# A fused attention and two-expert kernel: the written order of all its steps made anew

## The chip, the cores and the metric

The kernel runs on one core of a Trainium2 chip. The metric is the device time of one execution in microseconds (us); below are the median and the ends of three executions. A core has five engines that run side by side, each in the order of its own program: TensorE (PE, matrix products; PEld is its weight loads), VectorE (DVE), ScalarE (ACT), GpSimd (POOL) and SyncE (SP), which here issues all DMA transfers. They wait for one another by semaphores, so that an instruction that waits holds up everything behind it on its engine.

## What is computed

Causal attention with a bias from running sums of `s`, over 4 batches of 8 heads, 576 rows and 64 columns, and then two feed-forward blocks over all 2304 rows of 512 columns. The reference, cut:

```
scores = np.matmul(q, k.transpose(0, 1, 3, 2)) / sqrt(64)
cum = np.cumsum(np.maximum(s, 0.0), axis=-1)
bias = -(cum[:, :, :, None] - cum[:, :, None, :])
scores = np.where(causal, -1e9, scores + np.minimum(bias, 0.0))
attn = softmax(scores);  x = attn @ v              # heads side by side: 2304 x 512
h = x @ w_in;  x2 = (h - tanh(h)) @ w_out          # expert 1, d_ff 2048
h = x2 @ w2_in;  solu = h * softmax(h)             # expert 2, d_ff 1024
out = (layernorm(solu) * g_ln) @ w2_out
```

The weights come as float64 and are turned into float32 on the chip.

## The kernel before

**Arithmetic.** A float32 factor is split into a high and a low part (`xh`, `xl` in the buffer `xb`; `wih` and `wil`; `woh` and `wol`), and a product is three matmuls: high by high, low by high, high by low. The low part is a difference (`lo`, L831 for the attention's output, `diff`, L313, for the weights). A weight tile comes in as float64 (`cd`, L390) and is turned into float32 by four integer steps on DVE (L399, L402, L405, L410) and one on ACT (L417); then ACT writes the high part (L294) and DVE the low part (L313).

**Attention.** It goes by jobs. A job is a head pair p with some of its nine units; a unit is 64 query rows of both heads. J0 to J3 are pairs 0 to 3 with units 1 to 4 (the first 256 rows), J4 to J7 are pairs 0 to 3 with units 5 to 9, and J8 to J19 are pairs 4 to 15 whole. For each unit PE makes the scores against the keys up to the diagonal (L715; a half of the array for each head) and adds the mask (L723); DVE adds the bias and finds the row's extreme (L732, in buffer `U`); ACT takes the exponential and its sum (L743); DVE guards and inverts the sum (L656, L659); POOL scales the row (L747); PE turns it by transposes against an identity (L781, `idn` or `idx`); ACT copies the turned block to `pt` (L294). When the units of a half are turned, PE weighs the values (L821), ACT and DVE write the result's high and low parts (L294, L831), and SP stores them to DRAM (L834). The bias of J0 to J3 is cumulated in place; that of all others is a table `cum_d` in DRAM, from which SP loads `bc` (L602). Keys come by L580, queries by L584, values by L588 and L590.

**Experts.** Expert 1 goes by nine blocks of 256 rows. Its width of 2048 is 16 slices f of 128; the first eight slices go over all blocks in two visits of four, with the partial sum kept in DRAM, and the last eight after that. For a slice, `h_part` (L868) is 12 matmuls, ACT takes the tanh (L873), DVE the difference, the high and low parts are written to `gh`, and `x2_part` (L891) is 12 matmuls into the bank `acc`. Block 0 takes its `xb` straight from J0 to J3. Expert 2 follows for each block (L1016, L1120, L1134), and the output goes out in L1169.

**What sets the order.** Every piece of work is a step with the engine (or the choice of engines) that may do it, its dependences and the buffers that it takes and frees; there are 3302. `Plan.order` goes through the table `ORDER`: a word in base 36 is three times the step's number plus the choice of engine, and `+n` is n filler matmuls on PE (`warm`, L558, on a tile of zeros `junk`) that yield nothing. The steps go to the engines in the table's order, so the table alone sets what stands ahead of what on each of them. A step's cost, as in `t_score` and `t_turn`, is not looked at on this way. There are 9 buffers `U`, 6 PSUM banks, 4 `bc`, 5 tiles each of keys and queries.

Of the kernel before, what the change touches and what calls it, by code (L numbers as in the profile page):

```python
# [43 lines left out]
TB = 256  # L44
# [5 lines left out]
0 f 3 u i l x 49 4i 7x p r +20 13 10 1u 2i 16 86 1a 1c 1x 39 bu 2l 4d 6 2p 1f 20 3c 4l 2r 23 1i 4f 1l 89 3f 2u 26 2x  # L50
29 bx 3i 81 +7 1o 3l 83 30 1r ff +1 2c 9 3o 2f +1 33 bl 36 +1 3r 3u +1 4r 31x 5i jc 4u 8f 3x 4y 50 5l 32l 8i 8m 5o 53
c 56 96 5r 8o 59 5u 66 8r 40 99 5x 9u 4o 43 9c al 8u 69 46 8x bp 6x 9x 6f a1 br c3 8c a3 5c 70 90 cu 5f a6 c6 c0 73 ca
di 6d a9 6i cx 60 ac 320 6l fc 76 ao e9 d0 6o 79 dl 63 7c af d3 cc 9f d6 9i 6r cf ar ec d9 7f ci f9 6u au 9l ax ef 323
+2 9o cl ei 7i el 93 b0 +2 7l 9r fi 32o 326 eo ai b3 7o 329 j9 co b6 er n9 7r dc cr b9 eu 32c r6 df dr 7u 32r fl bc du
32u 32f bf gc 32x hi 32i dx 330 bi e0 gf 333 fo 339 gi fs 336 jf fu hr fx j6 +7 ji +1 k9 hl g0 ho gl g3 v3 hu gr 11o
gp dp +4 g6 n6 gu hx e3 gx h0 i0 e6 i3 g9 +4 ex h9 if r3 33c h3 hc i6 h6 +1 ii 33f hf v0 33i i9 f0 35x il f3 33l +1 io
ic 3cl ir 33o 33r f6 ki iu 3co km 33u ko n3 jl 3cr jr 33x kc lf 3cu ju jp jx kf 3cx 50l k0 nf kr ix ku lo l6 k3 j0 189
# [1260 lines left out]
```

## Time and profile before

| | us |
|---|---|
| median of three runs | 781.94 |
| lowest, highest | 779.62, 782.77 |
| the profiled execution | 778.94 |
| its span in the trace | 777.2 |
| PE busy | 764.8 (98% of the span) |
| DVE, ACT, POOL busy | 565.0, 409.8, 119.5 |

An engine is busy while it works on an instruction; PE's fillers count as busy too. In a row of the trace the first two numbers are the start and the length, then come the engine, the line, the operation, what it writes and reads, and its shape; a bracket at the end gives the idle time just before and what ended it. The granted clock of PE is 1.00 of full speed in every window. Outside its span the profiled execution has 1.74 us.

### The profile page before, as it was taken

Reading aid. Unit: us, or ns where it says so; the run is one execution under the profiler, and the core shown is the slowest. Engines: PE = TensorE matmul, PEld = TensorE weight load, DVE = VectorE, ACT = ScalarE, POOL = GpSimd, SP = SyncE. Lnnn points to the kernel's source line nnn. Section 1 sums busy time; section 2 is a strip of 40 time slices with the busy share of each in tenths; the row PEclk is TensorE's granted clock in tenths of the full one; section 3 lists DMA queues with packets and bytes.
Section 4 is the critical chain, followed back from the end, with each engine's and each line's share of the span. In section 5 each row is a group of like instructions: output and inputs, shape, how many; then the busy total and the mean of one; then the engine's idle time right before and its main releaser. Section 6 shows DMA issues by size and latency. Waiting matters only on the chain.

```text
span 777.2 us, 16641 instructions
## 1 busy us (share of the span) xinstructions
PE 764.8 (98%) x6239; PEld 676.8 (87%) x6239; DVE 565.0 (73%) x1647; ACT 409.8 (53%) x1030; POOL 119.5 (15%) x193
## 2 busy tenths in 40 slices
PE   8899999999999999999999999999999999999997
PEld 5566788879889899999999898898888899989986
DVE  6888989654564458786699998869496755586783
ACT  6789989775665545454465663423243332343431
POOL 3235354431230200000000000001020001010000
PEclk9999999999999999999999999999999999999999
DMA  7999979874444278876535522112000310110001
GB/s 202 293 302 257 316 235 314 258 209 158 154 140 155 85 252 266 262 261 215 180 123 181 167 83 55 35 48 82 28 28 28 96 55 14 42 55 28 20 36 41
DMA packets 90033, 111.90 MB, mean 144 GB/s; under 512 B 11792, under 2 KB 74256, under 8 KB 89952
## 3 DMA queue, kind: packets, MB, share of 16 engines
q1 hardware_dynamic: 89952, 110.83, 46.2%
q8 instruction: 49, 0.80, 0.4%
q14 instruction: 32, 0.26, 0.1%
HBM read 87.11 MB, written 23.70 MB: 143 GB/s over the span
## 4 chain that ended last, share of the span: by engine, by line
PE 88%; DVE 5%; ACT 2%; DMA 2%; issue 1%; SPq 1%; POOL 0%; DVEq 0%; ACTq 0%; POOLq 0%
PE t L868 23%; PE big L891 13%; PE t L1134 12%; PE acc L891 11%; PE t L821 6%; PE big L1016 6%; PE t L781 5%; PE t L715 5%; PE b L1016 4%; PE t L1120 2%; ACT U L743 1%; DMA bc<-cum_d 1%; DMA cum_d<-pt 1%; ACT pt L294 1%; DVE U L732 1%
## 5 line engine op out<-in xcount | busy, mean ns | idle before, releaser
L868 PE MATMUL t<-xb,wih 128*128 128x256 f32 x1152 | 202.5, 279 | 0.0
L868 PEld LDWEIGHTS t<-xb,wih 128*128 128x128 f32 x1152 | 175.0, 188 | 1.7 <-DVE r L656 0.2
L868 PE MATMUL t<-xb,wil 128*128 128x256 f32 x576 | 159.5, 277 | 0.0
L868 PEld LDWEIGHTS t<-xb,wil 128*128 128x128 f32 x576 | 108.3, 188 | 0.0
L747 POOL TENSOR_SCALAR U<-U,r 128x64 f32<-128x64 f32 (+8 forms) x144 | 82.8, 589 | 163.5 <-DVE r L659 50.2
L891 PE MATMUL acc<-gh,woh 128*128 128x256 f32 x576 | 102.6, 280 | 0.8 <-DVE xp L953 0.7
L891 PE MATMUL big<-gh,woh 128*128 128x256 f32 x576 | 101.0, 278 | 0.0
L873 ACT ACTIVATE th<-t 128x256 f32<-128x256 f32 x144 | 54.7, 381 | 77.1 <-PE t L868 69.7
L877 DVE TENSOR_TENSOR g<-t,th 128x256 f32<-128x256 f32 x144 | 59.5, 417 | 46.6 <-ACT th L873 45.3
L294 ACT CAST gh<-g 128x256 fp32r<-128x256 f32 x144 | 58.1, 406 | 65.1 <-DVE g L877 32.4
L743 ACT ACTIVATE U<-U,m 128x64 f32<-128x64 f32 (+8 forms) x144 | 80.1, 558 | 21.2 <-DVE m L732 20.7
L891 PEld LDWEIGHTS big<-gh,woh 128*128 128x128 f32 x576 | 87.8, 188 | 1.0
L891 PEld LDWEIGHTS acc<-gh,woh 128*128 128x128 f32 x576 | 87.0, 188 | 1.7 <-ACT th L873 0.8
L891 PE MATMUL acc<-gh,wol 128*128 128x256 f32 x288 | 79.8, 277 | 0.4 <-DVE wol L313 0.4
L891 PE MATMUL big<-gh,wol 128*128 128x256 f32 x288 | 79.9, 277 | 0.0
L313 DVE TENSOR_TENSOR gh<-g,gh 128x256 fp32r<-128x256 f32 x124 | 54.0, 439 | 28.2 <-ACT gh L294 27.1
L732 DVE CUSTOM_DVE_ANT_0 U<-bc,t 128x64 f32<-128x64 f32 (+8 forms) x144 | 60.2, 441 | 8.3 <-PE t L723 6.6
L314 POOL TENSOR_TENSOR gh<-g,gh 128x256 fp32r<-128x256 f32 x20 | 16.5, 827 | 316.9 <-ACT gh L294 249.6
L294 ACT COPY pt<-t 128x512 f32<-128x512 f32 (+4 forms) x160 | 60.0, 428 | 7.2 <-PE t L781 6.4
L715 PE MATMUL t<-kn,q 64*64 64x288 f32 (+8 forms) x640 | 58.9, 422 | 2.3 <-DVE wol L313 1.3
L891 PEld LDWEIGHTS acc<-gh,wol 128*128 128x128 f32 x288 | 54.1, 188 | 0.6 <-DVE wol L313 0.6
L891 PEld LDWEIGHTS big<-gh,wol 128*128 128x128 f32 x288 | 54.2, 188 | 0.0
(114 smaller groups left out, 1433.8 us busy)
## 6 DMA issues: line engine op xcount, KB each, us to landing
xb<-xd SPq DMA_DIRECT2D x17, 1024.0 KB, 6.1
cd<-in_moe_w_in_dram SPq DMA_DIRECT2D x24, 512.0 KB, 4.8
cd<-in_moe_w_out_dram SPq DMA_DIRECT2D x24, 512.0 KB, 5.0
bc<-cum_d SPq DMA_DIRECT2D x32, 288.0 KB, 6.4
pd<-xp SPq DMA_DIRECT2D x18, 512.0 KB, 3.8
xp<-pd SPq DMA_DIRECT2D x18, 512.0 KB, 3.6
xd<-xs SPq DMA_DIRECT2D x16, 320.0 KB, 4.5
kn<-in_k_dram SPq DMA_DIRECT2D x16, 288.0 KB, 6.6
```

Source lines behind the costliest of these rows:

```text
L294: then(nc.scalar.copy(o, i) if scale == 1.0 else nc.scalar.activation(out=o, in_=i, func=AF.Copy, scale=scale))
L313: return self.any([("dve", t_dve(n, pair=True), lambda: nc.vector.tensor_tensor(*views(), op), "diff-dve"), ("pool", t_pool(n) + split, la ...
L715: nc.tensor.matmul(X[a][c, :z - a], lhsT=V["q"][r, o:o + 64], rhs=V["k"][r, a:z], start=True, stop=True, skip_group_check=True)
L732: nc.vector.tensor_tensor_reduce(out=X["u"][:, a:z], in0=V["bc"][:, n, a:z], in1=X[b][:, a - b:z - b], scale=-0.125, scalar=X["m"] if "m" ...
L743: nc.scalar.activation(out=X["u"][:, :nk], in_=X["u"][:, :nk], func=AF.Exp, scale=-1.0, bias=X["m"], accum_out=Y["s"][:, n:n + 1])
L747: eng.tensor_scalar(X["u"][:, :nk], X["u"][:, :nk], Y["r"][:, n:n + 1], 1.0, ALU.mult, ALU.mult)
L868: nc.tensor.matmul(ps, lhsT=w[l][:, k, f * 128:f * 128 + 128], rhs=xb[:, r, k, :], start=k == 0 and x == 0, stop=k == 3 and x == 2)
L873: nc.scalar.activation(out=X["th", f], in_=X["h", f], func=AF.Tanh)
L877: nc.vector.tensor_tensor(X["g", f], X["h", f], X["th", f], ALU.subtract)
L891: nc.tensor.matmul(X["acc"][:, m, :], lhsT=w[l][:, f, m * 128:m * 128 + 128], rhs=X["gh", f][:, r, :], start=f == c0 and m % 2 == 0 and x ...
L1016: i = nc.tensor.matmul(o, lhsT=self.x2[j][:, l, x, k], rhs=r[:, b, k, :], start=start and k == 0 and n == 0, stop=k == 1 and n == 2, skip_ ...
L1134: nc.tensor.matmul(X["po"], lhsT=X["lt", k // 4][:, l, k % 4, :], rhs=r[:, k, :], start=k == 0 and a == 0, stop=k == 7 and a == 2)
```

## The change

The table is replaced by another one with the same 3302 steps, and the cost figures in the steps' descriptions are replaced too: those of a score of one part or two, of a turn of one to four blocks, of the weighing (2353 and 801 become 2165 and 685 ns), of an expert-1 part (1370 becomes 1372) and of an expert-2 part (1366 becomes 1380). Since the order is read from the table, the new costs change no instruction. The table's first and last lines and the costs:

```diff
 ORDER = """
-0 f 3 u i l x 49 4i 7x p r +20 13 10 1u 2i 16 86 1a 1c 1x 39 bu 2l 4d 6 2p 1f 20 3c 4l 2r 23 1i 4f 1l 89 3f 2u 26 2x
+0 u 3 i l f x 10 49 7x p r +20 13 4i 1u 16 86 2i 1a 1c 1x bu 39 1f 20 2l 6 1i 23 4d 3c 4l 1l 2r 26 4f 89 3f 29 +4 1o
...
 def t_score(n, rows):
-    t = 1.6667 * n + 119.0 if rows == 1 else {192: 393.0, 320: 599.0, 448: 868.0, 576: 1090.0}[n]
+    t = 1.6667 * n + (160.0 if n < 128 else 180.0 if n < 256 else 150.0) if rows == 1 else {192: 535.0, 320: 685.0, 448: 912.0, 576: 1150.0}[n]
...
-                s = add("pe", t_turn(128, c1 - c0), turn, [t, X["pad"]] + ([] if start else [self.pt_first[g]]),
+                s = add("pe", t_pe({1: 104.0, 2: 226.0, 3: 300.0, 4: 436.0}[c1 - c0], 128 * (c1 - c0)), turn, [t, X["pad"]] + ([] if start else [self.pt_first[g]]),
...
-        s = self.add("pe", t_pe(2353.0 if g else 801.0, 2712 if g else 880), mm, deps, acq=("ps",),
+        s = self.add("pe", t_pe(2165.0 if g else 685.0, 2712 if g else 880), mm, deps, acq=("ps",),
```

The fillers become 46 (53 before). The visits that PE pays to the half-array work of L715 and L821 between pieces of full width become 42 (39 before). Two copies and two other small steps go over to POOL, and five differences that POOL made go to DVE (258 there, 253 before).

Three places follow where the order around J4 and J5, the first jobs on the loaded bias, is another.

PE from J4's last scores to its first turns, with J3's weighing (of `pt_538` before, `pt_550` after), before and then after, filler and mask rows left out:

```order
L715 MATMUL t<-kn,q 64x512 x2
L715 MATMUL t<-kn,q 64x288 x4
...
L715 MATMUL t<-kn,q 64x320 x2
...
L715 MATMUL t<-kn,q 64x384 x2
L715 MATMUL t<-kn,q 64x448 x2
...
L781 MATMUL t<-idn,U 128x128 x5
...
L821 MATMUL t<-pt_538,v 64x256 x2
L821 MATMUL t<-pt_538,v 64x128 x2
```

```order
L821 MATMUL t<-pt_550,v 64x256 x2
L821 MATMUL t<-pt_550,v 64x128 x2
...
L715 MATMUL t<-kn,q 64x512 x2
L715 MATMUL t<-kn,q 64x288 x4
...
L715 MATMUL t<-kn,q 64x320 x2
...
L715 MATMUL t<-kn,q 64x384 x2
L715 MATMUL t<-kn,q 64x448 x2
...
L868 MATMUL t<-xb,wih_95 128x256 x2
L868 MATMUL t<-xb,wil_96 128x256
...
L781 MATMUL t<-idn,U 128x128 x6
```

J3's last turn and its weighing moved ahead of J4's scores, and the first `h_part` (eight matmuls on `wih_95` and four on `wil_96`), which stood behind all of J4's turns, moved ahead of them; the first `x2_part` moved ahead of J4's weighing.

DVE at J4's first reductions (the L732 rows on loaded `bc`; `wil_96` and `wol_98` are the low parts of the first two weight tiles), before and then after:

```order
L831 TENSOR_TENSOR xb<-t,xb 128x256
L405 SCALAR_TENSOR_TENSOR ct<-cd,ct 128x512
L313 TENSOR_TENSOR wil_96<-ct,wih_95 128x4x128
L659 RECIPROCAL r<-r 128x1
L410 SCALAR_TENSOR_TENSOR ct<-cd,ct 128x512
L732 ISA U,m<-bc,t 128x384
L732 ISA m 128x1
L732 ISA U,m<-bc,t 128x320
L732 ISA m 128x1
L738 MEMSET U 128x64
L313 TENSOR_TENSOR wol_98<-ct,woh_97 128x512
```

```order
L405 SCALAR_TENSOR_TENSOR ct<-cd,ct 128x512
L831 TENSOR_TENSOR xb<-t,xb 128x256
L313 TENSOR_TENSOR wil_96<-ct,wih_95 128x4x128
L410 SCALAR_TENSOR_TENSOR ct<-cd,ct 128x512
L831 TENSOR_TENSOR xb<-t,xb 128x256
L313 TENSOR_TENSOR wol_98<-ct,woh_97 128x512
L732 ISA U,m<-bc,t 128x320
L732 ISA m 128x1
L732 ISA U,m<-bc,t 128x384
L732 ISA m 128x1
```

J3's low part (the second L831) and the low part of the first `w_out` tile now stand ahead of J4's first reduction; J3's last inversion (L659) has moved up, ahead of J1's low part.

PE at J5's turns, from J5's scores of units 8 and 9 on, before and then after:

```order
L715 MATMUL t<-kn,q 64x512 x2
L715 MATMUL t<-kn,q 64x288 x4
...
L715 MATMUL t<-kn,q 64x320 x2
...
L781 MATMUL t<-idn,U 128x128 x3
L891 MATMUL acc<-gh,woh_97 128x256 x2
...
L781 MATMUL t<-idn,U 128x128 x3
L868 MATMUL t<-xb,wih_95 128x256 x2
...
L715 MATMUL t<-kn,q 64x384 x2
L715 MATMUL t<-kn,q 64x448 x2
...
L781 MATMUL t<-idx,U 128x128 x4
L781 MATMUL t<-idn,U 128x128 x4
```

```order
L715 MATMUL t<-kn,q 64x512 x2
L715 MATMUL t<-kn,q 64x288 x4
...
L715 MATMUL t<-kn,q 64x320 x2
...
L715 MATMUL t<-kn,q 64x384 x2
L715 MATMUL t<-kn,q 64x448 x2
...
L781 MATMUL t<-idn,U 128x128 x3
L868 MATMUL t<-xb,wih_95 128x256 x2
...
L781 MATMUL t<-idn,U 128x128 x3
L781 MATMUL t<-idx,U 128x128 x4
L781 MATMUL t<-idn,U 128x128 x4
```

The `x2_part` is gone from between the scores and the turns of units 8 and 9, and J6's scores of units 6 and 7 stand ahead of J5's first turns.

On SP the load of J4's keys, which stood ahead of the two `bc` loads from `cum_d`, now stands behind them and one load of queries:

```order
L602 DMA bc<-cum_d 64x1152 x2
L584 DMA q<-in_q_dram 128x320
L580 DMA kn<-in_k_dram 128x576 x2
```

The loads ahead of that pair (the table of sums, its store, the first jobs' operands) keep their places but for a swap or two.

## Rows read from the trace of the kernel before

**Rows 1.** The page's first part: busy us, share of the span, instructions.
```profile
PE 764.8 (98%) x6239; PEld 676.8 (87%) x6239; DVE 565.0 (73%) x1647; ACT 409.8 (53%) x1030; POOL 119.5 (15%) x193
```
**Rows 2.** Busy time of each engine by stretch, of its length given first.
```profile
core 0: us, PE busy (x) PEld busy (x) DVE busy (x) ACT busy (x) POOL busy (x), PEclk, DMA share, GB/s
0.00:20.00 20.00, 17.43 (x157) 11.22 (x159) 13.04 (x79) 12.87 (x49) 8.29 (x28) 1.00 0.71 203
20.00:40.00 20.00, 17.80 (x176) 12.03 (x173) 17.03 (x57) 14.68 (x42) 5.55 (x10) 1.00 1.05 300
40.00:60.00 20.00, 18.83 (x175) 13.59 (x176) 16.46 (x61) 16.69 (x42) 8.12 (x12) 1.00 1.06 291
60.00:80.00 20.00, 19.48 (x218) 12.72 (x217) 17.18 (x84) 19.17 (x63) 10.31 (x18) 1.00 0.96 258
350.00:400.00 50.00, 50.00 (x444) 50.00 (x443) 36.57 (x77) 22.87 (x52) 1.66 (x2) 1.00 0.56 187
```
**Rows 3.** The chain that ended last, 0 to 80 us: start, us, what.
```profile
12.86 5.76 DMA cum_d<-pt
...
19.21 6.44 DMA bc<-cum_d
```
**Rows 4.** Instructions from 15 to 28 us; brackets give idle time before and releaser.
```profile
17.88 0.51 SPq L580 DMA_DIRECT2D kn<-in_k_dram  x1
...
18.68 1.13 SPq L602 DMA_DIRECT2D bc<-cum_d  x2
...
21.51 0.87 PE L821 MATMUL t<-pt,v 128*64 128x256 f32 x8
...
21.96 0.85 SPq L584 DMA_DIRECT2D q<-in_q_dram  x2
...
22.93 0.93 PE L715 MATMUL t<-kn,q 64*64 64x320 f32 x6 [0.54 <-DMA kn<-in_k_dram]
...
23.02 0.41 DVE L831 TENSOR_TENSOR xb<-t,xb 128x256 fp32r<-128x256 f32 x1
...
24.87 0.71 POOL L747 TENSOR_SCALAR U<-U,r 128x192 f32<-128x192 f32 x1 [4.25 <-DVE r L659]
...
25.33 0.62 ACT L294 CAST woh<-ct 128x512 fp32r<-128x512 f32 x1 [2.01 <-DVE ct L410]
...
25.81 0.55 DVE L732 CUSTOM_DVE_ANT_0 U<-bc,t 128x384 f32<-128x384 f32 x1 [0.52 <-DMA bc<-cum_d]
26.78 0.63 DVE L313 TENSOR_TENSOR wol<-ct,woh 128x512 fp32r<-128x512 f32 x1
```
**Rows 5.** PE from 20 to 36 us by line: busy, mean ns, idle before.
```profile
L558 PE MATMUL acc<-junk 128*128 128x256 bf16 x18 | 3.0, 274 | 0.0
```
**Rows 6.** PE's instructions at the end of J4's turns.
```profile
29.79 0.71 PE L781 MATMUL t<-idn,U 128*128 128x128 f32 x5
...
34.51 0.48 PE L868 MATMUL t<-xb,wih 128*128 128x256 f32 x2
```
**Rows 7.** POOL and PE at J5's units 8 and 9.
```profile
43.30 1.57 POOL L747 TENSOR_SCALAR U<-U,r 128x512 f32<-128x512 f32 x2 [2.50 <-DVE r L659]
...
44.46 0.65 PE L781 MATMUL t<-idx,U 128*128 128x128 f32 x4
```
**Rows 8.** PE's instructions from 100 to 103.1 us.
```profile
100.44 0.28 PE L868 MATMUL t<-xb,wil 128*128 128x256 f32 x1
100.65 1.20 PE L715 MATMUL t<-kn,q 64*64 64x512 f32 x12
...
101.90 0.48 PE L868 MATMUL t<-xb,wih 128*128 128x256 f32 x2
102.22 0.28 PE L868 MATMUL t<-xb,wil 128*128 128x256 f32 x1
102.33 0.39 PE L868 MATMUL t<-xb,wih 128*128 128x256 f32 x2
...
102.68 0.39 PE L868 MATMUL t<-xb,wih 128*128 128x256 f32 x2
```

More of the change, by code (lines that the diff above doesn't have):

```diff
@@ new lines @@
+37f 1if 1lu 1bo 1fx 1lx 1br 1h6 1g6 1cl 1m0 1g4 1ii 1m3 1hc 1cu 1g9 1io 1co 3ei 1cx 1gc 1ls 37i 1iu 1gf 1h0 37l 1m6
+1h3 3eu 1go 1hf 3el 1hi 37o 3f9 1hu 3eo 1m9 37r 1is 1ha 37u 3ex 1il 1mc 1hl 3f0 3fc 1ix 1j0 1gr 3f3 3ff 3b9 1j3 1ho
+1ml 3fi 3fo 1mf 1mp 1gu 3f6 1mr 1jc 1mi 3fl 3g3 1hr 1mu 3fr 1mx 3fu 1n0 3fx 1d0 1n9 3g0 380 1gi 1yl 1d3 3gl 1gl 1yi
+383 1d6 1d9 386 1jl 1dc 389 1df 1ru 1i3 38c 1jo 1nc 38f 253 3g6 38l 1ju 1jr 38i 256 3bc 1di 1jx 3h3 1dl 3g9 3bf 1yf
+1k0 1do 3gc 1s6 1k3 3gf 3bi 1n3 3h6 1dx 1k6 1dr 3h9 1nf 1n6 3go 3hc 3gi 1ki 1du 1i6 3bl 1e6 1e0 1e9 1k9 1i9 3gr 1e3
@@ new lines @@
+1s9 1ic 1sd 3hf 1sf 3bo 1ni 1si 3gu 39x 1sl 1so 1yr 1ec 1nr 3gx 38o 1nl 1nx 1nv 38r 38u 3br 38x 1no 1sr 1s3 1hx 1ef
+3bu 3ic 1su 1i0 1ei 390 1el 1jf 1o0 393 1o3 3bx 1kl 1yu 1of 1z0 1j6 1yy 3jc 1kr 396 1kc 1ko 1o6 1p0 1j9 1z3 1z6 1kf
+1z9 1ji 1zi 1p9 1ku 20o 3a0 1zl 1pf 1kx 3a3 3j3 20x 1zo 3a6 213 211 1p3 20r 1p6 1pd 1zr 1o9 1yo 1zv 1oi 1pi 1zx 3a9
+3hi 1ol 200 3ac 1oc 1l0 203 1pl 3al 1l3 3af 20f 1q6 3ai 1l6 3hl 3c0 1px 3ho 1oo 20u 2br 1q9 3hr 1po 1q0 1or 216 1qf
+206 1zc 1qc 1ou 3hx 219 3hv 1qi 1zf 3c3 1q3 21l 1ql 1ox 20i 3c6 3iu 21c 1qo 20l 2bo 1qr 3i0 3c9 1r3 3i3 1sx 3i6 250
@@ new lines @@
+24c 236 10c 24f 10f 22x 24i 10i 3l6 239 230 246 10r 3l0 3l9 3l3 3lx 3m0 24l 3m9 3lc 3mc 3mf 10u 3lf 110 10l 3mi 3li
+10x 113 10o 3mx 3ml 3mo 3mr 3nf 3mu 3n0 3no 1u3 3n3 3n6 1vl 1u6 3n9 1uc 1wr 1u9 1vo 3nd 1ui 1ug 1vu 279 1vr 2vf 1vy
+1ul 1wu 116 1w0 2vi 27c 1wx 27i 27m 1uo 27o 1w3 1x0 1ur 1w6 1x3 27f 24o 2bu 1w9 27r 119 27u 11c 1x6 27x 11f 1x9 1xc
+1v0 2or 1xo 280 24r 1v3 24u 1uu 283 1xf 1wc 1v6 2if 1xr 1ux 1wi 1xi 1wf 24x 1xu 1v9 286 1xl 3q9 1wl 1vc 1vf 2ci 1xx
+1wo 289 1vi 3o0 28c 2cl 1y0 3of 3o3 3o6 3o9 2co 3oc 3oi 2du 3ol 2cr 2fc 2cx 2cu 2dx 2d3 2e3 2ii 2j9 2e0 2e7 2fl 1y3
@@ new lines @@
+2e9 2jc 2ec 2fr 2ji 2ef 2d6 2fp 2d9 2er 2jo 2ff 2jf 2jm 2d1 2jr 2dc 2fi 2il 28f 2ju 2p0 2ip 2k6 2fu 1y6 2fx 2eu 1y9
+2ir 2g0 3ou 28i 2iu 1yc 2ix 2ex 28l 2jx 28o 2g9 3pc 3ox 2dl 3p0 2j0 2ei 2do 3si 3pf 2gc 2g3 2dr 2gf 2j3 2el 2k0 3ni
+2eo 2k3 2g6 2j6 2gi 3oo 3or 3pi 28r 2gl 2p3 2gr 2go 2k9 28u 3nl 2p6 2kc 2pa 2gu 28x 290 2vc 2gx 29x 3nr 2pc 3p3 2vo
+296 2h0 2df 3nu 2a6 3p7 3qc 2h3 2di 2a0 2hf 299 2a3 2pf 29c 2pi 294 3qr 2a9 29f 2ac 2pl 2h6 2ho 2af 3qf 29i 2ai 3qu
+3qi 2hi 29o 2hr 29l 2h9 2vr 2al 2hl 29r 2vv 2hc 2f0 3q0 2au 29u 2wf 2f3 2xl 2f6 2vx 2wi 2f9 2w0 2hu 2wl 2wo 2w3 2xo
@@ L161 @@
+7mx 7n0 7n3
 """
@@ L906, in expert1 @@
             if f < c1:
-                s = add("pe", t_pe(1370.0, 12 * TB), lambda f=f: h_part(f), ld + [w["ready"][2 * f]] + list(deps), acq=("ps",),
+                s = add("pe", t_pe(1372.0, 12 * TB), lambda f=f: h_part(f), ld + [w["ready"][2 * f]] + list(deps), acq=("ps",),
                         rel=("xb",) if f == c1 - 1 else ())
@@ L921, in expert1 @@
                 f2 = f - 2
-                s = add("pe", t_pe(1370.0, 12 * TB), lambda f=f2: x2_part(f), [glo[f2], w["ready"][2 * f2 + 1]],
+                s = add("pe", t_pe(1372.0, 12 * TB), lambda f=f2: x2_part(f), [glo[f2], w["ready"][2 * f2 + 1]],
                         acq=("acc",) if f2 == c0 else (), rel=("gh",))
@@ L1022, in pe @@
         def pe(go, deps, acq=(), rel=()):
[L1023 removed]
+            s = add("pe", t_pe(1380.0, 3072), go, deps + list(self.w2_all), acq=acq, rel=rel)
             s.after = [self.h2_last] if self.h2_last else []
@@ L1157, in expert2 @@
         for n in range(2):
-            a = add("pe", t_turn(128, 4), lambda n=n: turn(n), [s], acq=("ps", LT[n]), rel=("ct",) if n else ())
+            a = add("pe", t_pe(395.0, 512), lambda n=n: turn(n), [s], acq=("ps", LT[n]), rel=("ct",) if n else ())
             a.mode = (1, 1)
```

202 lines of the change are left out of this document (90 added, 112 removed).

## Prediction

> **What bounds the kernel now.** I read the busy shares first: PE is busy for 764.8 us of 777.2, 98%, and the next engine, DVE, for 73% [rows 1]. So PE is the bound, and only two things can move the end: time in which PE waits or runs fillers, and time that its own work takes. Both orders hold the same useful PE work, and the granted clock is 1.00 throughout [rows 2], so the size of that work is not in question. Where PE waits is read from the windows [rows 2]: it is idle for 2.6 us of the first 20, for 2.2 from 20 to 40, for 1.2 from 40 to 60 and for 0.5 from 60 to 80; later, as from 350 to 400, for nothing. From 80 us on the order can thus only cost, through the visits to half-array work (below); what it can win lies before 80 us, and there the visible idle of 20 to 80 us, 3.9 us, is not the whole, since fillers count as busy: from 20 to 36 us alone 18 of them stand in waits, with 3.0 us of busy time [rows 5].
>
> The chain of waits tells why PE waits there. The table of sums is stored from 12.86 us on, taking 5.76 us, and SP then issues the `bc` loads, which land 6.44 us after 19.21 [rows 3]. J4's first reduction on DVE starts at 25.81, after 0.52 us of idle time that this transfer ended [rows 4]. J4's first turns follow at 29.79, and the first `h_part` only at 34.51, when the turns are done [rows 6]. From J4 on the jobs hang on each other by the nine buffers `U` and on ACT and DVE, which are busy for 16.46 to 19.17 of each 20 us from 40 to 80 [rows 2]. So a gain of PE work placed in one wait comes out at the end only if the next job's chain does not give it back.
>
> **The change, part by part.** The sum is made against the profiled execution, 778.94 us (span 777.2 and 1.74 outside it), which is 3.0 below the median of 781.94; the differences are then laid on the median. The store of the sums keeps its place on SP but for swaps, so 12.86 and 25.65 stand in both orders.
>
> *J4's wait takes in the first `h_part`.* In before PE has scores, 18 fillers and transposes to do until 34.51 [rows 5, 6]. In after the twelve matmuls of `h_part` stand ahead of J4's turns, in place of fillers. Three matmuls of such a part take 0.35 us (102.33 to 102.68 [rows 8]), twelve 1.40. They lie in time in which PE waits anyway, so behind J4's turns 1.40 us less is left to do: minus 1.4, if J4's turns come no later.
>
> *J4 starts a little later.* Two things now stand in front of its first reduction. First its keys: SP issued them at 17.88, and the scores that waited for them began at 22.93, 5.05 us later [rows 4]. Now they are issued behind the `bc` pair (18.68 and 1.13 us) and one of the query loads (half of 0.85), so at 20.24 at the earliest; plus 5.05 this is 25.29, plus about 0.75 from the first score to a masked block, 26.0. Second DVE's own queue: J3's low part and `wol` stand ahead. `wol` needs ACT's cast of the high part, which ended at 25.95 (25.33 and 0.62), and takes 0.63 [rows 4]; as in before that gives 26.6. The conversions ahead of it move up a little (one L405 now stands ahead of J2's low part), so I take 26.1, near the keys' value, 0.3 later than 25.81. It is not more at the end of the job, because `wol` no longer stands between J4's reductions (26.78 [rows 4]). The term is plus 0.3, between minus 0.3 (`wol` out of the way decides) and plus 0.8 (26.6).
>
> *J5's turns are asked for earlier.* PE's work between J5's scores of units 8 and 9 and their turns loses the `x2_part`, 1.40 us. Those turns cannot come earlier by themselves: POOL scales the two units from 43.30 to 44.87, the first of them done after half of that, at 44.09, and the turn starts at 44.46 [rows 7]. That is 0.4 us of slack. So PE waits there for 1.40 less 0.4, plus 1.0. If the slack is not usable the price is 1.4; if J5's whole chain comes earlier it is nothing, which is the first rival.
>
> *From J6 on.* By J5's and by J6's weighing PE has been given exactly the same work in both orders, but for the fillers, seven fewer in after; they stand in waits, and I count nothing for them. If one of them stood in PE-bound time it would be worth at most the 0.27 us of its length [rows 5].
>
> *Visits to half-array work.* They are 42 instead of 39. The row after a visit begins shows 0.21 us from the last full-width matmul to the first score (100.44 to 100.65), where two such matmuls are 0.11 apart (102.22 to 102.33); on the way back two `wih` matmuls take 0.32 (101.90 to 102.22) where they take 0.24 else (0.35 less 0.11) [rows 8]. That is 0.18 a visit and 0.5 for three. Visits that fall into waits cost nothing, so the bounds are 0 and 0.5; most of PE's time has no waits, so I take 0.5. The Trainium skill speaks against the change here: "TensorEngine Tiling (Array Packing)", section Key Properties, says that changing the tiling mode drains TensorE. The 0.18 us of the rows agrees, and the page gives no price that would change the sum.
>
> *Engines off the path.* Five differences go from POOL to DVE, four small steps to POOL. They count nothing: PE's work covers them where it has no idle time, as from 350 to 400 us, where DVE is busy for 36.57 us of 50 [rows 2]. If that cover were gone, five times the 0.63 us of `wol` [rows 4] would be 3.2 us; nothing in the rows lets them all stand on the path.
>
> Sum: minus 1.4, plus 0.3, plus 1.0, plus 0.5 is plus 0.4 us: 779.3 for an execution like the profiled one, **782.3** on the median. No change that a measurement could tell: for this kernel about 0.5%, 3.9 us, is what one can tell from none, that is 778.0 and 785.9.
>
> **Rivals.**
> *1. The chain of J5 to J9 comes earlier too (faster).* If J5's buffers are freed earlier because PE does J4's weighing earlier, nothing is paid back at J5, and the tighter order also closes the visible idle time of 20 to 80 us: minus 1.4, plus 0.3, minus 3.9, plus 0.5 is minus 4.5, so 777.4. For it speaks that PE, not DVE or ACT, is the releaser of some waits there; against it that ACT is busy 19.17 of 20 us from 60 to 80 and DVE 17.18 [rows 2], so these jobs have no room to come together by 4 us.
> *2. DVE's queue holds J4 (slower).* J3's low part stands ahead of J4's first reduction. In before J3's last scaling ended at 25.58 (24.87 and 0.71), and from the weighing to the end of the low part J2 took 1.92 (21.51 to 23.43) [rows 4]. If J3's scaling still ends at 25.58, then a turn and its copy (0.6), 1.92 and `wol`'s 0.63 put J4's first reduction at 28.7, 2.9 late instead of 0.3. That adds 2.6: plus 3.0, so 784.9, or 785.3 with 1.4 at J5. It decides from the point where J3's scaling ends after 23.0 (26.1 less 0.63, 1.92 and 0.6), and every further microsecond is one in the time. For it: the move in the order is there. Against it: J3's inversion has moved up on DVE, so that its scaling should end well before 24.
> *3. J6 to J9 pay as J5 does (slower).* From 46 to 72 us I find hardly any slack between a unit's scaling and its turn. If each of these four jobs also has its PE work moved ahead of the place where it filled the wait, each pays J5's 1.0 again: plus 0.4 and 4.0, so 786.3. Against it: by J6's weighing the same work has been given, so only the order within a job can do it.
> *4. The new table does nothing.* Orders on engines that are not waited for may differ without effect. This is the forecast's own value within its bounds, 781.9, and has no chance of its own.
>
> **How the numbers follow.** The forecast with its bounds (minus 1.4, minus 0.3, 0 and 0 give 780.2; minus 1.4, plus 0.8, 1.4 and 0.5 give 783.2) has 0.42. Rival 1 has 0.25, 0.23 of it below 778.0. Rival 2 has 0.19, a third of it above 785.9, where J3's scaling ends even later. Rival 3 has 0.14. So faster by over 0.5% 0.23, slower 0.20, within 0.5% the rest, 0.57. The range goes from rival 1 to rival 3, each with the 0.8 us by which the highest run stands off the median (782.77 against 781.94): 776.6 to 787.1. Outside are some 0.05 below and 0.07 above.
>
> **What would show each step.** In the trace of after: J4's first L732 at 26.1 or a little later, with J3's L831 and `wol` done before; at 28 or later it is rival 2. The keys' load issued at about 20.2 and landed by 25.3. The first `h_part` done before J4's first turn, and fewer than 18 fillers between 20 and 36 us. A wait of PE for POOL or DVE of about 1.0 us ahead of J5's turns of units 8 and 9; if it is not there and PE's idle time from 40 to 80 us is under 1 us, rival 1 is right; if such waits stand ahead of the turns of J6 to J9 too, rival 3. A switch of 0.2 at the added visits. What would make the prediction wrong without a rival: a wait after 80 us, where before has none.

## The result, and the profile after

The changed kernel takes 786.47 us in the median of 14 runs (783.87 to 789.48) where the kernel before takes 781.86 (14 runs on the same chip): a ratio of 1.0062, 95% interval 1.0038 to 1.0086. A second comparison gave 786.11 against 782.63, 1.0042 (1.0023 to 1.0062). So it is slower by 0.4 to 0.6%, some 4 us, where I had forecast 782.3 and no change. The time lies inside the range, near its upper end. The profiled execution has 783.87 us and a span of 782.1.

The page's first part, and the busy time by stretch (first the length, then each engine's busy time and instructions, the granted clock, the DMA share and GB/s), which answer [rows 1] and [rows 2]:

```profile
PE 765.9 (98%) x6232; PEld 676.2 (86%) x6232; DVE 561.1 (72%) x1634; ACT 411.6 (53%) x1028; POOL 121.8 (16%) x208
```

```profile
0.00:20.00 20.00, 15.67 (x154) 10.30 (x154) 12.52 (x74) 11.41 (x43) 8.15 (x27) 1.00 0.69 204
20.00:40.00 20.00, 18.55 (x175) 12.42 (x176) 16.67 (x58) 15.56 (x46) 7.21 (x10) 1.00 1.06 306
40.00:60.00 20.00, 16.80 (x171) 11.64 (x162) 15.54 (x56) 15.73 (x40) 9.19 (x12) 1.00 1.01 266
60.00:80.00 20.00, 18.70 (x195) 12.16 (x195) 17.83 (x81) 18.84 (x61) 9.76 (x18) 1.00 0.94 247
...
350.00:400.00 50.00, 50.00 (x444) 50.00 (x443) 26.45 (x58) 19.42 (x44) 0.74 (x1) 1.00 0.47 162
```

PE's idle time went up from 2.6 to 4.3 us in the first 20, down from 2.2 to 1.5 in the next 20, up from 1.2 to 3.2 from 40 to 60 and up from 0.5 to 1.3 from 60 to 80. From 350 to 400 us both orders are alike.

These windows don't hold the same work in both orders, so I made a table of places where they do: points in PE's program at which both orders have given PE the same steps. The table has the start of PE's next step after such a point, less the same in the profiled execution of before, in us; what a stage costs is the difference of two columns. The points are named by before's own time. "Front" is the new table up to a point and the old one after it, "rest" the reverse (experiments below).

| trace | 23 | 36 | 48 | 71 | 99 | 273 | 346 | 421 | end |
|---|---|---|---|---|---|---|---|---|---|
| before, a second trace | +0.34 | +0.46 | +0.86 | +0.85 | +0.84 | +0.80 | -0.35 | -0.14 | -0.10 |
| after | +1.13 | -0.68 | +0.29 | +2.59 | +2.40 | +6.30 | +4.93 | +4.93 | +4.97 |
| after, a second trace | +2.42 | +0.61 | +1.57 | +3.87 | +3.68 | +8.06 | +9.14 | +12.07 | +12.76 |
| front, to 48 us | +1.77 | -0.02 | +0.95 | +2.02 | +2.03 | +2.10 | +2.25 | +2.53 | +2.03 |
| rest, from 48 us | +0.33 | +0.05 | +0.17 | +2.63 | +2.43 | +5.55 | +4.03 | +4.02 | +4.64 |
| front, to 101 us | +2.26 | +0.45 | +1.41 | +3.69 | +3.50 | +3.42 | +2.00 | +4.59 | +4.20 |
| rest, from 101 us | +0.20 | +0.21 | +0.21 | +1.73 | +2.21 | +6.89 | +6.21 | +6.21 | +6.64 |

For the profiled execution of after: +0.3 up to 48 us, +2.3 from 48 to 71, -0.2 from 71 to 99, +3.9 from 99 to 273, and -1.3 behind that, together +5.0; the medians differ by 4.6. The last item is not the order's: before's own second trace has -0.9 there.

**The start, to 23 us.** The rows of POOL and PE, of before and then of after (start, length, engine, line, what, and in brackets the idle time before and what ended it):

```profile
0.73 0.31 POOL L553 MEMSET junk<- 128x256 bf16 x1 [0.29 <-POOLq L1291]
...
1.10 4.45 PE L558 MATMUL acc<-junk 128*128 128x256 bf16 x20 [1.10 <-POOL junk L553]
5.48 0.48 PE L715 MATMUL t<-kn,q 64*64 64x64 f32 x4
```

```profile
2.75 0.31 POOL L553 MEMSET junk<- 128x256 bf16 x1
...
3.12 3.86 PE L558 MATMUL acc<-junk 128*128 128x256 bf16 x20 [3.12 <-POOL junk L553]
6.90 0.33 PE L715 MATMUL t<-kn,q 64*64 64x64 f32 x4
```

The zeros that the fillers read are written 2.02 us later, because POOL now makes the identity and the masks first. PE's 20 opening fillers wait for the zeros, and J0's first scores stand behind the fillers: 1.42 us later. SP's store of the sums follows the first jobs: it was issued at 12.96 us here, and at 13.62 and 14.26 in two other traces with the new front, against 12.86 [rows 3].

**J4's wait, 23 to 36 us.** SP, PE and DVE in after, answering [rows 4 to 6]; one fence for each:

```profile
20.49 0.91 SPq L580 DMA_DIRECT2D kn<-in_k_dram  x2
```

```profile
25.07 0.87 PE L821 MATMUL t<-pt,v 128*64 128x256 f32 x8 [0.19 <-ACT pt L294]
...
26.09 0.93 PE L715 MATMUL t<-kn,q 64*64 64x320 f32 x6
...
30.14 0.50 PE L868 MATMUL t<-xb,wih 128*128 128x256 f32 x2
...
31.62 0.82 PE L781 MATMUL t<-idn,U 128*128 128x128 f32 x6
...
35.00 0.66 PE L781 MATMUL t<-idn,U 128*128 128x128 f32 x4
```

```profile
26.39 0.42 DVE L831 TENSOR_TENSOR xb<-t,xb 128x256 fp32r<-128x256 f32 x1
27.04 0.69 DVE L313 TENSOR_TENSOR wol<-ct,woh 128x512 fp32r<-128x512 f32 x1 [0.23 <-ACT woh L294]
27.65 0.48 DVE L732 CUSTOM_DVE_ANT_0 U<-bc,t 128x320 f32<-128x320 f32 x1
```

J4's first reduction comes at 27.65 us instead of 25.81, behind J3's low part and `wol`; the first `h_part` (30.14) fills the wait ahead of the first turns (31.62), and the last turns start at 35.00. Of the 18 fillers of [rows 5] 13 are left.

**J5.** PE and POOL, answering [rows 7]:

```profile
45.38 0.66 PE L781 MATMUL t<-idn,U 128*128 128x128 f32 x4 [1.16 <-POOL U L747]
46.52 0.74 PE L781 MATMUL t<-idx,U 128*64 128x128 f32 x5 [0.48 <-POOL U L747]
```

```profile
44.63 1.83 POOL L747 TENSOR_SCALAR U<-U,r 128x512 f32<-128x512 f32 x2 [1.46 <-DVE g L877]
```

PE waits twice for POOL's scaling of units 8 and 9, 1.16 and 0.48 us.

### The profile page after: what moved, and what is told of

Read it like the earlier page. It is cut to its first block, busy times and chain, and to the rows that moved or that the text cites. A ratio compares the mean times of both kernels' runs of the same rounds, so it can differ in the third digit from the quotient of the medians.

```text
span 782.1 us, 16630 instructions
## 1 busy us (share of the span) xinstructions
PE 765.9 (98%) x6232; PEld 676.2 (86%) x6232; DVE 561.1 (72%) x1634; ACT 411.6 (53%) x1028; POOL 121.8 (16%) x208
## 4 chain that ended last, share of the span: by engine, by line
PE 90%; DVE 5%; ACT 3%; issue 1%; POOL 1%; DVEq 0%; POOLq 0%; ACTq 0%
PE t L868 24%; PE big L891 12%; PE acc L891 12%; PE t L1134 12%; PE big L1016 6%; PE t L821 6%; PE t L781 5%; PE t L715 5%; PE b L1016 4%; PE t L1120 2%; ACT U L743 1%; DVE U L732 1%; PE acc L558 1%; PE t L723 0%; POOL U L747 0%
## 5 line engine op out<-in xcount | busy, mean ns | idle before, releaser
L747 POOL TENSOR_SCALAR U<-U,r 128x512 f32<-128x512 f32 (+8 forms) x144 | 84.6, 601 | 133.7 <-DVE r L659 55.6
L743 ACT ACTIVATE U<-U,m 128x576 f32<-128x576 f32 (+8 forms) x144 | 80.0, 558 | 20.5 <-DVE m L732 20.0
L732 DVE CUSTOM_DVE_ANT_0 U<-bc,t 128x256 f32<-128x256 f32 (+8 forms) x144 | 60.0, 442 | 5.9 <-PE t L723 4.9
L715 PE MATMUL t<-kn,q 64*64 64x288 f32 (+8 forms) x640 | 59.1, 421 | 0.2
```

Of the source, the lines that this page charges most:

```text
L715: nc.tensor.matmul(X[a][c, :z - a], lhsT=V["q"][r, o:o + 64], rhs=V["k"][r, a:z], start=True, stop=True, skip_group_check=True)
L732: nc.vector.tensor_tensor_reduce(out=X["u"][:, a:z], in0=V["bc"][:, n, a:z], in1=X[b][:, a - b:z - b], scale=-0.125, scalar=X["m"] if "m" ...
L743: nc.scalar.activation(out=X["u"][:, :nk], in_=X["u"][:, :nk], func=AF.Exp, scale=-1.0, bias=X["m"], accum_out=Y["s"][:, n:n + 1])
L747: eng.tensor_scalar(X["u"][:, :nk], X["u"][:, :nk], Y["r"][:, n:n + 1], 1.0, ALU.mult, ALU.mult)
```

## Experiments

All hybrids keep the kernel's code and change only words of the table. The ratios are to the kernel before, run beside each on the same chip, with the 95% interval.

**Which stage costs.** The new table up to a point at which PE has been given the same work, then the old one's other words in their order; and the reverse. Twice, with the cut at J5's weighing (48 us) and at 101 us.

```diff
 # front_after_to_48; front_after_to_101 alike with a later cut
-ORDER = (the old table)
+ORDER = (the new table up to J5's weighing) + (the old table's words that are not yet used)
 # rest_after_from_48; rest_after_from_101 alike
-ORDER = (the old table)
+ORDER = (the old table up to J5's weighing) + (the new table's words that are not yet used)
```

> The new order up to J5's weighing (48 us), the old order from there on; the two orders have given PE the same work at that point. In the trace of the new order this point comes 0.3 us later than before, but J6's weighing 1.9 later and the point at 73 us 2.6 later. Theory C (J4's late start is carried down the chain of J5 to J8 on DVE, ACT and POOL): the point at 73 us is again 2 to 2.6 us late, and the whole is slower than before by 2 to 2.6. Rival R (J6 to J8 lose by their own new order): 0.3 late at 73 us, and within 0.5 of before at the end.

> The old order up to J5's weighing, the new one from there on. Theory C: nothing lost by 73 us, 2.4 us lost between 101 us and the end, so slower than before by 2 to 2.6. Rival R: 2.3 us lost between 48 and 73 us, and slower than before by 4.5 to 5.

> The new order up to 101 us, where PE has again been given the same work, the old order from there on. If the loss after 101 us belongs to the order there (its visits to half-array work are 20 instead of 15): slower than before by 2.4, all of it present at 101 us. If it is the late arrival that costs again later: slower by 4 to 5.

> The old order up to 101 us, the new one from there on. If the five more visits cost about 0.5 us each, as the means of PE's steps in the two traces suggest: plus 2.4. If a visit costs 0.18, as the prediction had it: plus 0.9. If the loss after 101 us comes from arriving late: nothing.

Measured: front to 48 us 1.0016 (0.9994 to 1.0038), rest from 48 us 1.0040 (1.0011 to 1.0068), front to 101 us 1.0037 (1.0009 to 1.0065), rest from 101 us 1.0047 (1.0021 to 1.0073). The intervals overlap; the traces, in the table above, part the stages better. The stage from 99 to 273 us costs 3.1 to 4.7 us in each trace that has the new order there and under 0.1 in the two hybrids that have the old one (front to 48 us, front to 101 us), whatever the front was. The new front up to 48 us costs 0.3 to 1.6. The stage from 48 to 71 us costs 2.3 to 2.5 with the new order. The old order costs nothing there in before's second trace, but +1.08 behind a new front and +1.52 in the last hybrid, which has the old table up to there. (One more trace with the old order from 99 to 273 us, `before_word_ahead` below, costs 0.89 there; 0.8 of it is the slow rhythm of the last section.)

**What the stage from 48 to 71 us hangs on.** The +1.08 is the front's. At the point at 53 us, between J6's turns, after is 1.39 behind and not 0.29 as at 48 us; these 1.1 us come up in every trace of the table with the new front, and 0.1 or nothing in those with the old one. J6's turns of units 7 and 6, before and then after:

```profile
52.44 0.60 PE L781 MATMUL t<-idx,U 128*128 128x128 f32 x4
```

```profile
53.26 0.66 PE L781 MATMUL t<-idx,U 128*128 128x128 f32 x4 [0.37 <-POOL U L747]
54.35 0.52 PE L781 MATMUL t<-idn,U 128*128 128x128 f32 x3 [0.44 <-DVE r L659]
```

With the old order behind the new front PE waits at the same place:

```profile
53.98 0.66 PE L781 MATMUL t<-idx,U 128*128 128x128 f32 x4 [0.44 <-POOL U L747]
```

J6's first reduction on DVE starts 1.4 us later in after (48.11 instead of 46.74), while PE is only 0.3 us behind. I read this as the rest of J4's price: what PE has won there is paid back not only at J5 but at J6 too, where its turns come up ahead of J6's own chain. The +1.52 of the last hybrid starts with a transfer that is late in that execution; its row is J7's first reduction, which before has at 55.19 without a wait:

```profile
56.06 0.62 DVE L732 CUSTOM_DVE_ANT_0 U<-bc,t 128x448 f32<-128x448 f32 x1 [0.58 <-DMA bc<-cum_d]
```

Of the 2.3 us that after loses from 48 to 71 there remain 0.1 ahead of J7, 0.4 at J7 (between the points at 58 and 60 us) and 0.7 at J8. With the old front and the new order behind it, the 2.46 are 0.2 ahead of J7, 1.6 at J7 and 0.7 at J8.

**The visits alone.** The old order, with 12 expert parts between 99 and 280 us moved by one to four PE places so that each cuts a run of half-array work in two: 12 visits more. Three of the 12:

```diff
-... 1k0 3a3 1i3 1s3 ... 1hx 1i6 3ic 1k6 1i0 ...
+... 1k0 3a3 3ic 1i3 1s3 ... 1hx 1i6 1k6 1i0 ...
-... 1sx 21c 263 1t0 ... 25l 1ro 3ix 21r 25o ...
+... 1sx 21c 3ix 263 1t0 ... 25l 1ro 21r 25o ...
-... 2j9 1wu 28f 2vi ... 2j3 2jo 3l6 2jm 2jc ...
+... 2j9 1wu 3l6 28f 2vi ... 2j3 2jo 2jm 2jc ...
```

> The old order with twelve expert-1 parts between 101 and 280 us moved by one to four PE steps so that each cuts a run of half-array work in two: 12 more visits, no instruction added. From 99 to 273 us the old order took 174.4 to 174.5 us in three traces. Theory V (a visit costs what the prediction took, 0.18, or a little more): this stretch takes 2.0 to 2.3 us more, the whole 0.3% more. Theory W (a visit costs 0.5, which would explain the new order's whole loss there by its five more visits): 6 us more, 0.8%. If visits cost nothing: 174.5.

Measured: 790.68 against 780.20, 1.0137 (1.0109 to 1.0165), 10.5 us. In the 12 short windows between the points of equal work around each cut, the cuts themselves cost 1.68 us together, 0.14 each (0.01 to 0.31). That is my 0.18 and not 0.5 or more. But the profiled execution loses 9.8 us from 99 to 275 us, so 8.1 us of them arose outside those windows: 3.6 are more waiting of PE (4.1 us from 99 to 273 us instead of 0.5), 0.8 the slow rhythm of the last section, and the rest lies in turns, scores and the ends of expert parts and was not followed. The longest waits of PE from 100 to 310 us (waiting line, waited for, us in total, times, the longest), of this kernel and then of before:

```profile
PE t L781 <- POOL U L747: 2.6, 4, 1.0
PE acc L891 <- DVE xp L953: 0.5, 1, 0.5
...
```

```profile
PE t L781 <- POOL U L747: 0.5, 1, 0.5
```

One of them, in PE's instructions behind the fourth cut:

```profile
146.16 0.28 PE L868 MATMUL t<-xb,wil 128*128 128x256 f32 x1
147.48 0.33 PE L781 MATMUL t<-idn,U 128*128 128x128 f32 x1 [1.04 <-POOL U L747]
```

An expert part that is moved by a few places no longer covers the time in which POOL scales the next row. So a visit is as cheap as I had it, and what stands between the scaling and the turn is not.

**Fewer ends of half-array runs.** A group of scores with another group behind it is cheaper in the traces than one with the weighing or full-width work behind it (units 4 and 5: 0.42 to 0.60 against 0.72 to 0.88 us), and the new order has 19 such ends against 15 between 99 and 280 us. Two kernels tried to win from that: PE steps moved by at most two places in the new order (22 words, to save 2.3 us by those prices) and by at most four in the old (11 words, 1.3 us). Two of the moves of each:

```diff
 # after_narrow_regrouped
-... 1ix 1j0 1gr 3f3 ... 1ml 3fi 3fo 1mf 1mp ...
+... 1ix 1j0 3fo 1gr 3f3 ... 1ml 3fi 1mf 1mp ...
-... 1pd 1zr 1o9 1yo ... 1zx 3a9 3hi 1ol 200 ...
+... 1pd 1zr 3hi 1o9 1yo ... 1zx 3a9 1ol 200 ...
 # before_narrow_regrouped
-... 1il 1gf 1ho 1ix 1mi 3fo 1g4 1go ...
+... 1il 1gf 3fo 1ho 1ix 1mi 1g4 1go ...
-... 2pu 2fl 3nf 2ei 1yc ... 2px 2eu 2do 2fu ...
+... 2pu 2fl 2ei 1yc ... 2px 2eu 3nf 2do 2fu ...
```

> The new order with PE steps between 101 and 280 us moved by at most two places, so that scores stand next to scores and the weighing next to full-width work; the number of visits falls only from 41 to 40. In the traces a group of scores that another group follows takes 0.2 to 0.3 us less than one that a weighing or full-width work follows. Theory G (what a step is followed by sets its price): this stretch takes 2.0 to 2.3 us less than the 177.6 to 179.1 of the new order in three traces. Theory W (only the number of visits counts): at most 0.5 us less. If the stretch is long because PE waits: no change, or longer.

> The old order with PE steps between 99 and 273 us moved by at most four places in the same way, visits 36 instead of 37. Theory G: this stretch takes 1.3 us less than 174.4, so 173.1, and the whole is 0.17% faster, at the edge of what can be told. Theory W: 0.3 us less. If PE's order there meets waits: no gain.

Measured: 794.80, 1.0195 (1.0164 to 1.0227), and 789.64, 1.0107 (1.0076 to 1.0139). From 99 to 273 us they cost +13.0 and +6.6 where after costs +3.9 and before nothing. The longest waits of PE from 100 to 290 us, first of the one made from after, then of the one made from before:

```profile
PE t L781 <- POOL U L747: 1.6, 2, 1.1
PE t L868 <- DVE m L732: 0.9, 1, 0.9
PE t L781 <- DVE m L732: 0.8, 2, 0.6
...
```

```profile
PE t L781 <- POOL U L747: 2.1, 3, 1.1
PE acc L891 <- ACT xp L294: 1.0, 1, 1.0
PE t L781 <- DVE m L732: 0.7, 2, 0.4
```

All waits of PE from 99 to 273 us are 5.5 and 4.9 us, where after has 0.9 and before 0.5; that is half of what the first kernel loses beyond after and two thirds of what the second loses. The gain, if there was one, is not to be seen under it, and the rest was not followed. Both say what the cuts said: small moves of PE work between 99 and 273 us open waits, though PE looks full there.

**J4's reduction earlier.** The changed order with the load of J4's keys ahead of the `bc` pair, J4's first scores ahead of J3's last copy and weighing, and its first reductions ahead of J3's low part and `wol`.

```diff
 # after_j4_early: words moved up
-... ax f9 d6 ... 329 fc 93 ... 339 df ... 330 f0 +1 fl jf f3 333 gc 336 f6 fo hi gf fu ...
+... ax fc f9 d6 ... 329 93 ... 339 fl gc df ... 330 fo gf f0 +1 jf f3 333 336 f6 hi fu ...
```

> The new order with J4's start set as in the old one: SP issues J4's keys ahead of the two bc loads, PE makes J4's first two score blocks ahead of J3's weighing, DVE makes the first two reductions ahead of J3's low part and of the first w_out difference. Theory C (J4's late start costs): J4's first reduction at 26.0 instead of 27.65, the turns of J4 end about 1.4 earlier, and the point at 73 us comes 1.5 us earlier than in the new order; the whole is 1.5 us faster than the new order. Rival R (J6 to J8 lose by their own order whenever J4 starts): J4 earlier, but the point at 73 us and the end as in the new order within 0.5.

Measured: 789.42, 1.0090 (1.0055 to 1.0125). The first reduction came to 27.27 us instead of 27.65 only. But this trace is 1.0 us later than after already at 23 us (+2.12 against +1.13), so that from this point on the reduction came 1.4 us earlier; and yet from 23 to 71 us the trace costs 1.38 where after costs 1.46. In this one trace J4's late reduction is thus worth next to nothing by 71 us, which is rival R. The total does not tell: its interval overlaps those of after, and the trace has slow stretches (below) from 273 to 421 us, +4.0.

**One conversion step at J7.** In the hybrid with the new order from 48 us, the loss from 48 to 71 us sits where PE waits for J7. DVE, ACT and PE of that hybrid, a fence each:

```profile
59.36 0.77 DVE L399 TENSOR_SCALAR ct<-ct 128x512 f32<-128x512 f32 x1 [0.91 <-ACT ct L417]
60.05 0.67 DVE L732 CUSTOM_DVE_ANT_0 U<-bc,t 128x512 f32<-128x512 f32 x1
```

```profile
58.66 0.67 ACT L417 ACTIVATE ct<-cd 128x512 f32<-128x512 f32 x1 [0.60 <-DMA cd<-in_moe_w_out_dram]
```

```profile
60.87 0.52 PE L781 MATMUL t<-idn,U 128*128 128x128 f32 x3 [1.98 <-DVE m L732]
```

DVE is idle for 0.91 us: its next step is a weight conversion that waits for ACT, which waited for a transfer, and behind that step stand J7's reductions of units 8 and 9, whose scores are done. PE's next turn needs a bank that these reductions free, and waits 1.98 us. Before, DVE had the reductions first:

```profile
58.09 0.69 DVE L732 CUSTOM_DVE_ANT_0 U<-bc,t 128x512 f32<-128x512 f32 x1
...
59.75 0.42 DVE L399 TENSOR_SCALAR ct<-ct 128x512 f32<-128x512 f32 x1
```

Two kernels test it: in the hybrid the steps L399 and L402 go behind J7's last reduction; and in before L399 alone goes ahead of the first.

```diff
 # rest_from_48_word_moved
-... so qc 35f 1lf t0 tc qf 1lc ti rx sr tf qi 35i t3 tl ql su ...
+... so qc 1lf t0 tc qf 1lc ti rx sr tf qi t3 tl 35f 35i ql su ...
 # before_word_ahead
-... 1lf qi tc ru ql qc ti 1lc tf t0 rx tl t3 qf 35f 35i su ...
+... 1lf qi 35f tc ru ql qc ti 1lc tf t0 rx tl t3 qf 35i su ...
```

> As rest_after_from_48 (the old order to 48 us, the new one after), but two conversion steps of a weight tile (L399 and L402, at 59 us) stand on DVE behind the reductions of J7's units 8 and 9 again, as in the old order, instead of ahead of them. In rest_after_from_48 the first of these reductions began at 60.05 instead of 58.09, and PE's next turn, which needs a PSUM bank that the reductions free, at 60.87 instead of 59.04; 2.46 us were lost between 48 and 73 us. Theory Q (that queue position loses the time): the reduction at 58.4, the turn at 59.3, and at most 1.0 us lost between 48 and 73 us; the whole 1.5 us faster than rest_after_from_48. Rival S (the late exponentials and scores of J7 lose it): the turn still after 60.5, and 2 us or more lost.

> The old order with one step moved: the conversion step L399 at 59.75 us stands on DVE ahead of the reductions of J7's units 8 and 9, as in the new order. It waits for ACT's L417, which ended at 58.3 in the old order's trace, and takes 0.8. Theory Q: the reduction begins at 58.9 instead of 58.09, PE's turn up to 0.8 us later, and 0.3 to 0.8 us is lost by 73 us; the total can't tell it from before. Rival S: nothing lost.

Measured, the hybrid with the words moved, DVE and PE and then PE's longest wait from 48 to 73 us:

```profile
57.41 0.69 DVE L732 CUSTOM_DVE_ANT_0 U<-bc,t 128x512 f32<-128x512 f32 x1 [0.17 <-PE t L723]
...
59.07 0.42 DVE L399 TENSOR_SCALAR ct<-ct 128x512 f32<-128x512 f32 x1
```

```profile
58.25 0.52 PE L781 MATMUL t<-idn,U 128*128 128x128 f32 x3 [0.43 <-DVE m L732]
```

```profile
PE t L781 <- DVE m L732: 0.4, 1, 0.4
...
```

The wait of 1.98 is 0.43, and the stage from 48 to 71 us costs 1.24 instead of 2.46; of that only 0.18 has come up by J6's weighing (60 us on before's scale), the rest at J8. So these two words are worth 1.2 us, half of the stage, between the one trace of this hybrid and the one of the other; what holds J8 I did not find. In before the word ahead makes the stage cost 1.38 where it cost nothing, 0.94 of it by J6's weighing; but this is the weaker half of the test, since in that execution a load of keys landed late at 23 us and cost 3.9 us ahead of this place, where the order is before's, and a late arrival alone had cost 1.08 here in a hybrid. The times cannot show the words' worth: 1.0039 (1.0008 to 1.0070) and 1.0012 (0.9987 to 1.0036), with 1.2 us inside either interval.

In after itself the same three rows stand, with a shorter wait since PE comes there later, having lost 1.1 us at J6's turns:

```profile
59.63 0.46 DVE L399 TENSOR_SCALAR ct<-ct 128x512 f32<-128x512 f32 x1 [0.19 <-ACT ct L417]
60.01 0.68 DVE L732 CUSTOM_DVE_ANT_0 U<-bc,t 128x512 f32<-128x512 f32 x1
```

```profile
60.84 0.52 PE L781 MATMUL t<-idn,U 128*128 128x128 f32 x3 [0.80 <-DVE m L732]
```

The turn starts at the same time in both (60.84 and 60.87), as the reduction does. So in after this place costs 0.4 us and not 1.6. No run moved the two words in after, so what they are worth there is not shown.

**The two kernels once more**, unchanged.

> The kernel before once more, unchanged: how far two traces of one order differ by stage. If the stages are steady: within 0.5 us of the first trace at 48, 73, 101 and 273 us of it. The kernel front_after_to_48 kept the length of the stretch from 101 us to 280 us within 0.1 us, while rest_after_from_101 lost 2.2 us by 101 us in the old order, so I expect up to 2 us by 101 us and at most 0.3 from there to 273 us.

> The changed kernel once more, unchanged. If the new order itself loses the time by stage: again 2.0 to 2.5 us between 48 and 73 us, 3 to 4.7 us more than the old order between 101 and 280 us, and slower than before by 0.4 to 0.9% in total.

Measured: 783.04 against 782.63, 0.9992 (0.9965 to 1.0018), and 786.11, 1.0042 (1.0023 to 1.0062). Their traces are the first and the third line of the table: stages of the same order repeat within 0.5 us from 23 to 273 us, the start within 1.3, and what lies behind 273 us within some 6.

No kernel here beat both.

## Why the prediction was right or wrong, step by step

That 786.5 us lies in the range is luck: the range reached up to rival 3 at 786.3, and the loss was made up otherwise. The forecast itself, no change, missed it. Two steps failed, that nothing is lost from J6 on (2.3 us were, up to 71 us) and that the order can cost behind 80 us only through the visits (3.9 us and not 0.5, in the profiled execution).

**"12.86 and 25.65 stand in both orders", and nothing is counted ahead of 20 us: wrong.** The start costs 1.0 to 2.4 us in every trace with the new front, and under 0.4 in those with the old one. The 20 fillers behind POOL's late zeros are the first thing to be late, and POOL's own first scalings follow; at 9 us after is 0.2 and its second trace 1.4 behind, and at 23 us 1.1 and 2.4. So the lateness begins at the zeros, and more comes up between 9 and 17 us. (The same 20 fillers take 4.45 us in before and in after's second trace and 3.86 in after's first, which is where these two part.) No run moved the zeros alone, so how much is theirs stays open.

**J4's wait, -1.4 and +0.3: the sign right, the size off, and for another reason.** J4's first reduction came 1.84 us late and not 0.3; what held it last is what rival 2 names, DVE's queue with J3's low part and `wol`. I had taken J3's low part to be done well before, but PE gave J3's weighing at 25.07 only. Yet the stage wins 1.8 us (1.79 to 1.81 in the four traces of the table with the new front, whatever their start) where I had 1.1, since J4's turns make half of the lateness up: the first starts at 31.62 instead of 29.79, but [rows 6] has the first `h_part`, behind the turns, at 34.51, and in after it is done before the turns and the last of these starts at 35.00, in a trace that is 1.1 late already. The keys, issued at 20.49 (forecast 20.24), set nothing; the scores stood behind J3's weighing.

**J5, +1.0: right.** +0.96 in all four traces of the table with the new front (36 to 48 us), and PE waits there for POOL, as foretold.

**"From J6 on ... I count nothing": wrong, by 2.3 us.** By J6's weighing the same PE work has been given, and I stopped there. But same work given is not same waits: PE came to J6's turns ahead of J6's chain on DVE, ACT and POOL and waited for POOL's scaling, as it had at J5, for 1.1 us. The hybrid with the old order behind the new front pays the same there, so this part comes with the front. It is rival 3's place and, at J6, its mechanism, but not its size (4.0): J7 pays 0.4 and J8 0.7. At J7 it is another mechanism: the order of DVE's own work had changed, and a conversion that waits for ACT, and ACT for a transfer, stands ahead of the reductions that hold PE's banks. Moving two words shows it where the front is the old one (1.6 us there); in after, by the rows above, it costs only what J6 has not cost already. What holds J8 is not found.

**The visits, 0.18 each: right as a price, wrong as all that the stretch pays.** The cuts measured 0.14. The Trainium skill, "TensorEngine Tiling (Array Packing)", section Key Properties, says that changing the tiling mode drains TensorE; the 0.14 us shows a small price that the page does not give. What failed is "From 80 us on the order can thus only cost, through the visits". That stretch costs 3.1 to 4.7 us, not 0.5. There are 5 visits more there (20 against 15; elsewhere some go), worth 0.7 to 0.9. From the two traces of each order, sums over the steps between 99 and 273 us: half-array steps take 61.15 us where they took 59.66 (+1.5, with 18 ends of score groups against 15); the last interval of an expert part, mostly ahead of a visit, loses 0.7 to 0.9 more; the gaps at the first matmuls of parts, waits among them (0.70 at an `x2_part` at 265 us of after, 0.49 at one at 268), take 1.0 more; matmuls that follow each other slowly (below) 0.6 to 1.0; turns 0.1 to 0.3 less. These add up to some 3.9. That this stretch of the new order costs it, the hybrids show; how it splits is a reading of the traces, and the one attempt to win back the first item failed. The slow matmuls may not be the order's: `before_word_ahead` has 0.8 us of them here under the old order.

**What was not in the sum at all:** that PE, busy for 20.00 of 20 us, is not out of reach of the others. I took 100% busy for cover, and had read the windows of before behind 80 us as free of idle time, though PE is idle there for 0.45 us from 140 to 160 us and for 0.80 from 300 to 350. The 12 cuts bring 8.1 us of lateness outside their own places, 3.6 of it waits of PE. Nor do the engines off the path differ by five differences: 28 go from POOL to DVE and 23 from DVE to POOL, five only on balance. And I had put the size of PE's own work out of question since the granted clock is 1.00 throughout; the two rhythms below change it by 5 us at that clock.

Of the rivals, 1 (the chain to J9 comes earlier) is refuted, since idle time from 40 to 80 us went up from 1.7 to 4.5 us; 2 has the right place but no loss; 3 has nearly the time, and its mechanism at one of its four jobs. My chance of 0.20 for slower was too low, since I gave costs only to places at which I had read a wait in before, and every such place was before 50 us.

## What to carry to other kernels

What the busiest engine wins at one job it can pay back at the next ones, if their chains on the other engines come no earlier: here 1.8 us won at J4, 1.0 paid at J5 and 1.1 at J6. Where an order is made anew, go through each in-order queue and not only through the busiest engine's: look for steps that wait on a transfer (conversions of loaded weights) and have come to stand ahead of steps that free another engine's banks or buffers. An engine that shows 100% busy may still have each of its steps just in time, so price a reordering in such a stretch by an experiment that moves a few steps, not by the price of a switch. And compare two orders at points where the same work has been given, with a second trace of each for the noise.

## What the runs showed of the hardware

**Two rhythms at the same clock.** Matmuls of full width that follow each other without a wait start every 113 ns or every 118, at a granted clock of 1.00 in both, and the rhythm stays for whole stretches. A window of after and then of its second trace, where both do only expert work:

```profile
360.00:380.00 20.00, 20.00 (x179) 20.00 (x179) 7.54 (x15) 5.79 (x13) 0.74 (x1) 1.00 0.36 129
```

```profile
360.00:380.00 20.00, 20.00 (x172) 20.00 (x171) 7.44 (x16) 6.58 (x15) 0.74 (x1) 1.00 0.39 136
```

The same program does 179 or 172 matmuls in 20 us, with PE busy throughout. From 273 to 421 us all 1177 intervals within expert parts are slow ones in the second trace, and 2 of them in the first. The same steps in PE's instructions, first of after, then of its second trace (from one row's start to the next row's are three matmuls):

```profile
361.97 0.39 PE L868 MATMUL t<-xb,wih 128*128 128x256 f32 x2
...
362.31 0.39 PE L868 MATMUL t<-xb,wih 128*128 128x256 f32 x2
```

```profile
360.96 0.40 PE L868 MATMUL t<-xb,wih 128*128 128x256 f32 x2
...
361.32 0.40 PE L868 MATMUL t<-xb,wih 128*128 128x256 f32 x2
```

Three take 0.34 us in the one and 0.36 in the other. From 273 to 421 us this parts the two traces of after by 5.2 us of the 5.4 by which they differ there (-1.38 and +4.01 against before's trace), more than the change itself. Much of the spread of 783.6 to 791.7 in ten runs of that kernel, and of 776.8 to 785.7 in ten of before, may come from it; a trace exists of one run of each ten only. The slow rhythm was seen in traces of both orders. What sets the rhythm is open: no run here was made to tell. A forecast of under 1% for this kernel has to be laid on a median of many runs, not on one profiled execution.
